# Block-causal attention followed by a gated MLP: V loaded in f32 and cast on Pool, weights issued in pieces, the last key block as a full tile

## Chip, cores and metric

One core of a Trainium2 chip. The metric is the device time of one execution in microseconds. The kernel before: 418.41 us (median of 3 runs, 418.2 to 418.69).

## The reference

```python
B, H, S, D = 8, 8, 576, 64                     # q, k, v: [8, 8, 576, 64] f32
mask = (arange(S)[:, None] // 64) >= (arange(S)[None, :] // 64)
attn = softmax(where(mask, q @ k.T / 8, -1e9)) # rows of a block of 64 see whole blocks
x = (attn @ v).transpose(0, 2, 1, 3).reshape(4608, 512)
h = x @ w_in                                   # w_in [512, 2048]
g = h * sigmoid(beta * h)                      # beta [2048]
out = g @ w_out                                # w_out [2048, 512], out [4608, 512] f32
```

## The kernel before

Work is cut into 32 attention units (a batch has four, each a pair of heads) and 9 row chunks of the MLP (512 rows each: 64 products with w_in, 64 with w_out). The program plans all of it once, on guessed durations: whenever an engine is free it takes the ready operation with the lowest `prio`. The result is a fixed order for each engine, with semaphores between them. What matters below:

```python
# TensorE takes attention first (prio 10*u + 0..5), MLP products only where none is ready
xp  = P.op("PE", ..., prio=10 * u + 5)                    # unit u, of 32
o   = P.op("PE", 4 * mm(512), fh, ..., prio=1000 + 100 * r + j)        # x @ w_in, row chunk r
o   = P.op("PE", 16 * mm(512), fo, ..., prio=1000 + 100 * r + 16 + w)  # g @ w_out
...
# V of a batch: six transfers by Pool, f32 to bf16 on the way, straight into one of two buffers Vn
for i in range(4):
    g.dma_start(Vn[t.slot][:, i, h0:h1, 0:64], v[b, h0:h1, 128*i:128*i+128, :].rearrange("h p d -> p h d"))
...
# E * V of one head: 15 products; the last key block (64 keys) uses smaller tiles
for i in range(5):
    for t in range(i + 1):
        m = 64 if i == 4 and t else 128
        r = slice(64*h, 64*h+64) if t == 4 else slice(0, 128)
        g.matmul(PS[0:m, ..., 65*i:65*i+65], eblk(te, t, i, h), Vn[Tv.slot][r, t, 2*c+h, 0:65], ...)
```

Q and K come by the SP queue in f32, through four staging buffers each, and are cast by Pool (DVE for batch 0). E holds the exponentiated scores; the unit's E*V product is the last big TensorE step of its attention.

The softmax here doesn't subtract the row's maximum and nothing guards it: scores larger than these inputs give would overflow.

## Time and profile before

| | before |
|---|---|
| median, span of the profiled execution | 418.41 us, 413.8 us |
| first E*V product, first MLP product | 28.47 us, 54.09 us |
| w_out landed | 70.4 us |
| E*V of unit 32 starts | 219.0 us |

The page, the stages of the start and the chain are in the prediction. One more view is needed later, busy time by stage; columns: window, length, busy time of PE, PEld, DVE, ACT and Pool with instruction counts, granted clock, DMA share (it can read above 1.00 and is used for comparison only), GB/s.

```profile
72.00:100.00 28.00, 27.38 (x293) 16.34 (x294) 9.57 (x25) 11.79 (x18) 11.88 (x22) 1.00 0.95 108
100.00:130.00 30.00, 28.52 (x398) 18.26 (x399) 21.61 (x50) 23.72 (x33) 20.93 (x42) 1.00 0.76 150
130.00:160.00 30.00, 28.43 (x429) 19.18 (x432) 22.06 (x55) 21.31 (x30) 23.83 (x44) 1.00 1.03 152
```

TensorE is busy for 84.3 of these 88 us, with the DMA engines at 0.76 to 1.03 beside it.

### The profile page before, as it was taken

The numbers are of one execution on the slowest core, as the hardware profiler recorded it, in microseconds if no ns is written. First come the engines' busy times: TensorE is split into PE (matmuls) and PEld (weight loads), VectorE is DVE, ScalarE is ACT, GpSimd is POOL, SyncE is SP. The second block draws the span as 40 slices with busy tenths as digits, with TensorE's granted clock in tenths as the row PEclk, the third lists the DMA queues.
The fourth block names the chain that finished last, engine by engine and source line by source line (L and its number), as shares of the span: only waits on it lengthen the run. The fifth ranks groups of instructions, "written<-read, shape, count | busy, mean of one in ns | idle before, by whom it ended". The sixth has DMA issues, their size and how long they took to land.

```text
span 413.8 us, 7477 instructions
## 1 busy us (share of the span) xinstructions
PE 379.6 (92%) x3006; PEld 201.5 (49%) x3041; DVE 195.7 (47%) x377; ACT 215.2 (52%) x309; POOL 129.6 (31%) x248
## 2 busy tenths in 40 slices
PE   2359998999999998999999999999999999999986
PEld 1136643565655665455555444444444444444432
DVE  2515567244768776683337407137054071370520
ACT  1143676236786766943485437256174272461721
POOL 8366789226678967930010000000000000000000
PEclk9999999999999999999999999999999999999999
DMA  7998999939497999900100020110100101101001
GB/s 179 253 224 174 191 220 187 96 109 141 121 140 205 158 136 202 78 2 27 53 25 2 27 77 0 53 51 2 76 26 27 76 0 52 51 2 76 25 28 76
DMA packets 60899, 37.73 MB, mean 91 GB/s; under 512 B 39856, under 2 KB 56256, under 8 KB 60864
## 3 DMA queue, kind: packets, MB, share of 16 engines
q0 software_dynamic: 42336, 8.92, 24.9%
q1 hardware_dynamic: 18528, 28.33, 23.2%
q8 instruction: 24, 0.39, 0.4%
q14 instruction: 11, 0.09, 0.1%
HBM read 36.71 MB, written 9.44 MB: 112 GB/s over the span
## 4 chain that ended last, share of the span: by engine, by line
PE 74%; ACT 10%; DMA 6%; DVE 4%; POOL 3%; issue 2%; POOLq 0%
PE PS L551 30%; PE PS L531 25%; PE PS L482 11%; ACT E L444 8%; DMA Vn<-in_v_dram 5%; PE PS L437 4%; PE PS L408 2%; PE PS L510 2%; ACT th L539 2%; DMA w_out<-in_moe_w_out_dram 2%; DVE xq L501 1%; POOL w_out L351 1%; DVE gT L543 1%; POOL Vn L370 1%; DVE QT L416 1%
## 5 line engine op out<-in xcount | busy, mean ns | idle before, releaser
L543 DVE SCALAR_TENSOR_TENSOR gT<-th,PS 128x512 bf16<-128x512 f32 x144 | 98.6, 687 | 118.2 <-ACT th L539 118.1
L531 PE MATMUL PS<-xT,w_in 128*128 128x512 bf16 x557 | 127.2, 381 | 2.8 <-DVE KT L416 0.9
L444 ACT ACTIVATE E<-PS 128x1024 bf16<-128x1024 f32 x96 | 94.8, 1034 | 67.1 <-PE PS L437 66.9
L551 PE MATMUL PS<-w_out,gT 128*128 128x512 bf16 x560 | 124.8, 379 | 4.8 <-issue 1.5
L539 ACT ACTIVATE th<-PS,beta 128x512 f32<-128x512 f32 x144 | 99.3, 693 | 27.9 <-PE PS L531 27.9
L551 PEld LDWEIGHTS PS<-w_out,gT 128*128 128x128 bf16 x576 | 55.7, 98 | 70.5 <-issue 2.0
L531 PEld LDWEIGHTS PS<-xT,w_in 128*128 128x128 bf16 x576 | 54.7, 98 | 66.7 <-issue 2.0
L560 ACT ACTIVATE ost<-PS 128x512 f32<-128x512 f32 x36 | 21.5, 597 | 100.4 <-PE PS L551 100.4
L482 PE MATMUL PS<-Vn,E 128*128 128x65 bf16 (+1 forms) x896 | 48.8, 202 | 5.4 <-DMA Vn<-in_v_dram 3.8
L482 PEld LDWEIGHTS PS<-Vn,E 128*128 128x128 bf16 (+1 forms) x896 | 38.4, 104 | 16.0 <-issue 5.4
L437 PE MATMUL PS<-QT,KT 64*128 64x64 bf16 (+5 forms) x384 | 41.6, 310 | 2.2 <-ACT E L444 1.4
L370 POOL DMA_DIRECT2D Vn<-in_v_dram x36 | 31.2, 905 | 7.5 <-PE PS L482 6.5
L450 POOL MEMSET E<- 64x128 bf16 x64 | 13.2, 206 | 54.0 <-ACT E L444 49.2
L501 DVE TENSOR_TENSOR xq<-PS,inv 128x320 bf16<-128x320 f32 x64 | 29.3, 486 | 0.0
L416 DVE COPY QT<-PS 128x576 bf16<-128x576 bf16 x32 | 24.1, 752 | 6.4 <-PE PS L408 5.9
L516 DVE COPY xT<-PS 128x576 bf16<-128x576 bf16 x32 | 14.5, 453 | 26.2 <-PE PS L510 26.1
L402 POOL CAST Qn<-Qs 96x768 bf16<-96x768 f32 x28 | 23.1, 824 | 9.7 <-PE PS L408 8.1
L493 DVE RECIPROCAL inv<-PS 128x5 f32<-128x5 f32 x64 | 8.4, 173 | 36.3 <-PE PS L482 35.9
L437 PEld LDWEIGHTS PS<-QT,KT 64*128 64x128 bf16 (+1 forms) x384 | 14.9, 100 | 21.0 <-issue 7.3
L416 DVE COPY KT<-PS 128x576 bf16<-128x576 bf16 x32 | 24.0, 750 | 1.9 <-PE PS L408 1.7
L402 POOL CAST Kn<-Ks 96x768 bf16<-96x768 f32 x28 | 23.1, 824 | 1.8
L408 PE MATMUL PS<-identB,Kn 96*128 96x96 bf16 x192 | 15.8, 227 | 7.8 <-DVE KT L416 4.6
(27 smaller groups left out, 142.9 us busy)
## 6 DMA issues: line engine op xcount, KB each, us to landing
Qs<-in_q_dram SPq DMA_DIRECT2D x32, 288.0 KB, 4.4
Ks<-in_k_dram SPq DMA_DIRECT2D x32, 288.0 KB, 4.5
out_dram<-ost SPq DMA_DIRECT2D x36, 256.0 KB, 2.0
Vn<-in_v_dram POOLq DMA_DIRECT2D x28, 128.0 KB, 4.1
w_in<-in_moe_w_in_dram POOLq DMA_DIRECT2D x16, 128.0 KB, 6.9
w_out<-in_moe_w_out_dram POOLq DMA_DIRECT2D x16, 128.0 KB, 5.0
Vn<-in_v_dram POOLq DMA_DIRECT2D x8, 64.0 KB, 16.9
Vn<-in_v_dram POOLq DMA_DIRECT2D x14, 32.0 KB, 3.3
```

Source lines behind the costliest of these rows:

```text
L370: z.append(g.dma_start(Vn[t.slot][:, i, h0:h1, 0:64], v[b, h0:h1, 128 * i:128 * i + 128, :].rearrange("h p d -> p h d")))
L402: return g.tensor_copy(nat[tn.slot][:], raw_[ts.slot][:].rearrange("p h j d -> p j h d"))
L408: z = g.transpose(PSb[:, pt.slot, 96 * i:96 * i + 96], nat[tn.slot][:, i, :, :].rearrange("p h d -> p (h d)"), identB[0:96, 0:96])
L416: return g.tensor_copy(dst[td.slot][:].rearrange("c (p j) -> c p j", j=6), PSb[:, pt.slot, 0:576].rearrange("c (j p) -> c p j", j=6))
L437: z = g.matmul(o, KT[tk.slot][r, 128 * t:128 * t + m], QT[tq.slot][r, q0:q1])
L444: return g.activation(E3[te.slot][:, g0, :, :], PS[:, ps.slot:ps.slot + 2, :], ACT.Exp, scale=0.125)
L482: z = g.matmul(o, eblk(te, t, i, h), Vn[Tv.slot][r, t, 2 * c + h, 0:65], start=(t == 0), stop=(t == i or (i == 4 and t == 0)), skip_group_ ...
L501: return g.tensor_tensor(xq[tx.slot][:, :, 64 * w:64 * w + 64], a, x, ALU.mult)
L531: z = g.matmul(PS[:, ph.slot, :], w_in[:, c, 128 * j:128 * j + 128], xT[:, c, row:row + RC], start=(c == 0), stop=(c == 3))
L539: return g.activation(th[tt.slot][:], PS[:, ph.slot, :], ACT.Tanh, scale=beta[:, j:j + 1])
L543: return g.scalar_tensor_tensor(out=gT[tg.slot][:, j, :], in0=th[tt.slot][:], scalar=1.0, in1=PS[:, ph.slot, :], op0=ALU.add, op1=ALU.mult)
L551: z = g.matmul(PS[:, po.slot, :], gT[tg.slot][:, j, 128 * w:128 * w + 128], w_out[:, j, :], start=(j == 0), stop=(j == NJ - 1))
```

## The change

The intent: start earlier (V no longer on Pool's queue, where it crept in beside Q and K; the loads in one queue; the weights behind the first Q, K, V), make E*V shorter (all 15 products in one tile shape), and let the first output rows follow w_out as it lands. The diff, cut:

```diff
+        Vs = [sb(f"Vs{i}", [128, 5, 8, 64], f32) for i in range(NQ)]
...
-                o = P.op("POOL", c, fv, deps=ones, tiles=[t], lat=c + 3000, prio=20 if b == 0 else 50 + b, ...)
+                o = ld["V", b, h0] = P.op("SP", 6 * 400, fv, deps=vzero, tiles=[ts], xfer=5000 * n,
+                         prio=(0.5 if h0 == 0 else 2.5) if b == 0 else 4 * b + 0.5 - 3 * (b > 1), ...)
+                def fw(g, e, ts=ts, t=t, h0=h0, h1=h1):
+                    return g.tensor_copy(Vn[t.slot][:, :, h0:h1, 0:64], Vs[ts.slot][:, :, h0:h1, :])
+                o = P.op("POOL", 300 + 2140 * n, fw, deps=[o, *ones], tiles=[ts, t], ...)
...
-                            m = 64 if i == 4 and t else 128
-                            r = slice(64 * h, 64 * h + 64) if t == 4 else slice(0, 128)
+                            o = PS[:, (pa if h == 0 else pb).slot, 65 * i:65 * i + 65]
+                            z = g.matmul(o, eblk(te, t, i, h), Vn[Tv.slot][:, t, 2 * c + h, 0:65],
+                                         start=(t == 0), stop=(t == i))
...
+        for w in win:  w.deps += [ld["Q", 3], ld["K", 3]]      # one issue per piece of 256 KB
+        for w in wout: w.deps += [ld["Q", 6], ld["K", 6]]
+        for u in range(4, NU):                                 # later Q, K, V wait for weight pieces
+            w = win[4:8] if u < 8 else wout[8:12]
+            for o in [ld["Q", u], ld["K", u]] + ([ld["V", u // 4, 0]] if u % 4 == 0 else []):
+                o.deps += w
...
+                parts = [(0, NJ)] if r or w > 2 else [(4 * a, 4 * a + 4) for a in range(4)]
```

The plan also models the transfers as one queue, so every engine's order changes. (Not in the diff's words, but of weight below: a V can now wait in Vs as well as in Vn, so up to four batches of V can be on the core, and from batch 2 on the `prio` of V puts it ahead of Q and K of the last two units of the batch before.)

## The prediction

> **What bounds the kernel now.** I read the page first (busy shares and slices), then a table by stage, then the chain of waits, then the time line of single products.
>
> ```profile
> span 413.8 us, 7477 instructions
> ...
> PE 379.6 (92%) x3006; PEld 201.5 (49%) x3041; DVE 195.7 (47%) x377; ACT 215.2 (52%) x309; POOL 129.6 (31%) x248
> ...
> PE   2359998999999998999999999999999999999986
> ...
> DMA  7998999939497999900100020110100101101001
> ```
>
> TensorE is full from the fourth slice (about 31 us) to the end; the DMA engines are full only in the first seventeen slices. So there are two places for a gain: how early TensorE gets going, and how much TensorE work there is. The stages, with columns length, busy time of PE, PEld, DVE, ACT and Pool, clock, DMA share and GB/s:
>
> ```profile
> 0.00:28.50 28.50, 9.06 (x77) 4.96 (x77) 10.51 (x17) 7.34 (x10) 19.22 (x40) 1.00 1.18 216
> 28.50:54.00 25.50, 25.25 (x250) 16.59 (x252) 13.30 (x30) 12.63 (x17) 16.26 (x34) 1.00 1.00 192
> ...
> 100.00:170.00 70.00, 65.25 (x948) 43.08 (x952) 50.35 (x120) 51.39 (x72) 52.63 (x97) 1.00 0.93 158
> ...
> 224.00:318.00 94.00, 93.53 (x429) 42.55 (x436) 40.28 (x59) 47.04 (x70) 0.00 (x0) 1.00 0.09 34
> ```
>
> The first 28.5 us hold only 9 us of TensorE work. The chain says what it waits for (start, length, what):
>
> ```profile
> 8.51 19.82 DMA Vn<-in_v_dram
> 28.33 0.14 issue
> 28.47 2.47 PE PS L482 x30
> ...
> 60.48 3.59 POOL w_out L351 x7
> 64.06 6.30 DMA w_out<-in_moe_w_out_dram
> 70.37 1.42 issue
> 71.78 3.40 PE PS L551 x15
> ```
>
> V is the gate of the start: its last piece, issued at 8.51, lands 19.82 us later. Then the E*V products (L482) run, the first MLP product (L531) comes at 54.09, and w_out, landing at 70.37, costs one more small wait. The second place is inside L482:
>
> ```profile
> 28.47 1.07 PE L482 MATMUL PS<-Vn,E 128*128 128x65 bf16 x14 [3.85 <-DMA Vn<-in_v_dram]
> 29.47 0.26 PE L482 MATMUL PS<-Vn,F 64*64 64x65 bf16 x1
> 29.66 1.09 PE L482 MATMUL PS<-Vn,E 128*128 128x65 bf16 x14
> ...
> 128.69 0.72 PE L482 MATMUL PS<-Vn,E 128*128 128x65 bf16 x14
> 129.34 0.21 PE L482 MATMUL PS<-Vn,F 64*64 64x65 bf16 x1
> 129.49 0.72 PE L482 MATMUL PS<-Vn,E 128*128 128x65 bf16 x14
> ```
>
> A head's 15 products take 129.49-128.69 = 0.80 us. The start times of single matmuls in this trace (56 such heads, 72 to 224 us) split it: ten steps of 31 ns from full tile to full tile, 124 ns from the last full tile to the first 64-column one, two steps of 44 ns, 123 ns into the 64x64 tile, 147 ns out of it: 311+124+88+123+147 = 793 ns. Before 54 us the same steps are 54, 175, 65, 174 and 193 ns: 1.21 us.
>
> **What the Trainium skill says.** (1) TensorEngine Tiling (Array Packing), Key Properties: changing the tiling mode drains TensorE. The trace agrees: the three mode changes of a head cost about 93, 92 and 116 ns over a plain 31 ns step. (2) TensorE: Matmul & The Clock Gate, Back-to-back issue gap: N/2.4+2.5 ns warm and N/1.2 ns cold, for 65 columns 29.6 and 54.2 ns. Both are in the trace (29 to 31, and 54). The page's warm-up after about 3.4 us of sustained work does not fit: from 28.5 to 54 us there is hardly a gap, yet the steps stay cold until the 512-column products start. The granted clock reads 1.00 throughout and does not show it. (3) DMA: Bandwidth & Descriptors, Queues, rings and completion order: each DMA engine takes queues in turn, packet by packet. The trace agrees that it hurts V: it writes 128-byte packets on the Pool queue beside 1536-byte packets of Q and K on the SP queue, so V got 0.04 of about 0.48 MB in a 2 us slice from 12 to 22 us. (4) Same page, SWDGE vs HWDGE vs iDMA: a cast during a transfer is possible only from Pool. So V on the SP queue must come as f32 and be cast by an engine.
>
> **The change, part by part.** *V by SP, cast on Pool.* Removed from Pool: 54 issues of V, 31.2+12.0 = 43 us. Added: a cast of 128x2560 per batch. The Q/K cast takes 824 ns for 768 columns, so 2560 take 2.75 us by the same slope; 8 batches make 22 us. Pool ends 21 us lighter, off the critical path. The transfer: Q, K and V become one queue in the order needed: Q0 K0, V of two heads, Q1 K1 Q2 K2, the rest of V, Q3 K3, and the weights only after that. Q0 and K0 landed at 4.57 and 5.59 us; undisturbed Q/K pieces of 0.295 MB landed every 1.1 to 1.3 us. V of two heads is one such piece (6.9 us), the rest of V is three. Alone on the engines (70 to 76 us) 128-byte packets moved 155 GB/s; at the same packet rate 256-byte ones would move 310, so V should be no worse than Q/K per byte. Nine pieces after 6.9 us at 1.2 us: K3 lands at 17.7 us. Behind it lie cast, transposes, copy, scores, three exps, products, division and transposes back: 0.6+0.8+0.75+0.6+3.4+1.7+1.4+1.2 = 10.5 us, from the cold times in this trace. The first MLP product comes at about 28 us instead of 54.1, if w_in (issued from 17.7, 16 issues of 0.57 us) has its first quarter by 23 us. That is 26 us of start.
>
> Not all of it is gain. By 54 us the old kernel has done 108 of 384 Q/K transposes and 76 of 384 score products; four units need 48 each. The other 60 and 28 cost 60*52 ns = 3.1 us and about 2.4 us warm and must now come later. Net: 26-5.5 = 20.5 us.
>
> *Full last tile.* The count stays at 30 products per unit; all three mode changes go. A head becomes 15*31 = 467 ns: 326 ns less on each of the 56 heads that ran warm, 18.3 us. Pure TensorE time in a stage where it has 65.25 of 70 us. The eight cold heads (3.2 us) lie in the start and are not counted twice. A full weight load costs nothing more: 101 ns for 128 columns against 105 to 114 for 64, beside the matmul.
>
> *First output rows in four parts, weights in pieces.* Removes the wait at 70.37: 1.4 us. *New memsets* on DVE and Pool: a few times 0.2 us before any data is there.
>
> Against it I set 3 us for new waits: Q/K of batch 1 are held until the second quarter of w_in has landed, and those of batch 2 until the third of w_out. Sum: 413.8-20.5-18.3-1.4+3 = 376.6 us of span. The timed median is 4.6 us above the profiled span (418.41 against 413.8): 381 us; I say 382.
>
> **Rivals.** (a) *Other engines become the bound of the attention stage.* From 100 to 170 us 457 products are 15.2 units of 4.6 us; with PE at 4.0 us a unit, DVE (3.3) and ACT (3.4) would be at 83 to 85%. For it: they are close, and the chain has 8.2% on the exps. Against it: MLP products fill any hole, and the output ones ask little of either. If the whole tile gain drowned: 400. (b) *DMA becomes the bound.* V as f32 is written at twice the bytes; a unit moves 0.885 MB, 221 GB/s at 4.0 us, and the start moved 232. Against it: a batch unlocks some 12 us of attention and 31 us of MLP for about 15 us of DMA, so only the first 70 us can starve: 12 MB (weights and batch 1) after 18 us at 230 GB/s land at 70, and the work unlocked by then (two input halves of 13.8 us and batch 1) lasts from 28 to about 68. If 256-byte packets move at only 155 GB/s, V takes 7.6 us a batch, and with the starving the result is 388 to 395. (c) *The start is given back*: the fixed order, planned on guessed landing times, makes TensorE, or Pool ahead of its weight issues, wait for the wrong thing, as K2's transposes held the first scores until 18.9 us here. Half the start lost: 392.
>
> **Range and chances.** The tile gain is measured step by step and sits on the bound; the start has the error. Centre 382; 374 if products warm earlier or waits are less, 395 if (b) or (c) takes half of the start. Even (a) stays over 2% ahead, so slower needs something unforeseen. Faster 0.95, same 0.035, slower 0.015.
>
> **What would show it.** Right: L482 in one form of 128*128, two heads in about 0.95 us warm; the first L482 near 12 us and first L531 near 28; w_out landed by about 55 us and no wait there; Pool near 108 us busy; TensorE's idle time after the first MLP product no more than before. Wrong: first L531 after 34 us; V landings of 7 us or more a batch; holes in TensorE between 30 and 70 us that end on Qs, Ks or w_out; L482 steps over 40 ns.

## The result, and the profile after

404.09 us (median of 4 runs, 402.52 to 405.02) against 418.31 (416.26 to 418.69) in the same rounds. Ratio 0.9666, 95% interval 0.9622 to 0.971: faster by 3.3%. Ratios are the mean time of one kernel's runs over that of the other's of the same rounds, so not quite the ratio of the medians quoted. Executions over 1.5% slower than the fastest of the same kernel are left out of the means. The direction was right; the time lies 9 us above the predicted range. The gain in span is 11.3 us where 37 were predicted.

The page after, and its groups of the new products and casts:

```profile
PE 365.3 (91%) x3003; PEld 188.3 (47%) x3041; DVE 196.2 (49%) x380; ACT 214.8 (53%) x308; POOL 107.4 (27%) x212
...
PE   3866999977988898899999999999999999999986
...
PEclk9985899988989999999999999999999999999999
DMA  6899989999999997000110110200100201102002
GB/s 176 178 137 211 216 119 206 231 255 261 241 202 272 214 261 182 2 2 2 51 56 2 52 52 2 78 26 28 73 6 28 78 2 52 52 2 78 26 29 78
...
L503 PE MATMUL PS<-Vn,E 128*128 128x65 bf16 x960 | 36.6, 198 | 8.0 <-POOL E L476 5.6
...
L402 POOL CAST Vn<-Vs 128x2560 bf16<-128x2560 f32 (+2 forms) x9 | 18.7, 2080 | 12.4 <-DMA Vs<-in_v_dram 12.1
```

The predicted pieces are there: one product form, Pool at 107.4 us (predicted 108). But the PE row has 7s and 8s from the 9th to the 17th slice, where nearly all were 9s before, and the clock row dips. By stage:

```profile
28.50:54.00 25.50, 19.83 (x110) 8.86 (x109) 12.30 (x22) 10.83 (x17) 10.32 (x16) 0.73 0.95 185
...
72.00:100.00 28.00, 23.17 (x276) 13.41 (x278) 13.74 (x34) 12.72 (x18) 16.19 (x24) 0.90 1.04 253
100.00:130.00 30.00, 25.92 (x391) 16.20 (x390) 20.69 (x49) 23.13 (x32) 19.70 (x35) 0.92 1.02 236
130.00:160.00 30.00, 26.90 (x461) 17.57 (x463) 22.68 (x55) 23.94 (x34) 22.15 (x41) 1.00 0.94 223
```

From 72 to 160 us TensorE is busy for 76.0 of 88 us, 8.3 less than before, part of it at half clock; the DMA engines are full and move 223 to 253 GB/s. The start, in TensorE's time line (start, length, instructions, and in brackets the wait before them):

```profile
13.71 1.83 PE L503 MATMUL PS<-Vn,E 128*128 128x65 bf16 x30
...
31.73 3.19 PE L560 MATMUL PS<-xT,w_in 128*128 128x512 bf16 x7 [0.95 <-DVE xT L536]
37.94 0.66 PE L432 MATMUL PS<-identB,Qn 96*128 96x96 bf16 x6 [3.02 <-POOL Qn L426]
38.40 3.61 PE L560 MATMUL PS<-xT,w_in 128*128 128x512 bf16 x8
...
47.45 3.63 PE L560 MATMUL PS<-xT,w_in 128*128 128x512 bf16 x16
```

E*V begins 14.8 us earlier than before and the MLP 22.4 us earlier. But eight MLP products take 3.61 us at 38.40, where sixteen take 3.63 at 47.45: half clock, recorded from 29.63 to 43.28 us.

**Where the time went.** Take the start of the E*V product of units 8, 16, 24 and 32 from the trace, and, from the fixed instruction order, how many of the 1152 MLP products stand before it. An MLP product takes 216 ns at full clock (the median step in these traces); deduct that, and what is left is the time each eight units of attention cost beyond the MLP work done meanwhile. For example units 9 to 16 before: 130.3-90.3 = 40.0 us with 152-112 = 40 products (8.6 us) between: 31.4 us. The four stages and the tail add up to the span less 248.8 us of MLP. Each run has one profile; those of e1, e2 and e5 are of their quickest execution, that of e8 of its slowest.

| net us | units 1-8 | 9-16 | 17-24 | 25-32 | tail | span | MLP products before unit 32 |
|---|---|---|---|---|---|---|---|
| before | 66.1 | 31.4 | 30.6 | 29.6 | 7.3 | 413.8 | 284 |
| after | 51.3 | 39.7 | 30.5 | 25.9 | 6.3 | 402.5 | 188 |
| gain | 14.8 | -8.3 | 0.1 | 3.7 | 1.0 | 11.3 | |
| predicted gain | 24.5 | 5.2 | 5.2 | 5.2 | 0 | 37.1 with -3 for waits | |

The predicted gains by stage are the prediction's own terms: 20.5 for the start, 1.4 for w_out, and 0.326 us for each head from unit 5 on (8 heads in the first column, 16 in each other). Attention now ends 31 us sooner, but with 96 fewer MLP products done by then, which is 20.7 us given back. The largest miss is units 9 to 16, which became slower. That is where to look.

What stands in the SP queue there (start, time in the queue's issuing, what):

```profile
71.53 6.25 SPq L388 DMA_DIRECT2D Vs<-in_v_dram  x4
77.82 1.78 SPq L392 DMA_DIRECT2D Vs<-in_v_dram  x2
...
80.29 0.43 SPq L420 DMA_DIRECT2D Qs<-in_q_dram  x1
80.76 0.47 SPq L420 DMA_DIRECT2D Ks<-in_k_dram  x1
...
83.34 6.15 SPq L388 DMA_DIRECT2D Vs<-in_v_dram  x4
89.54 1.78 SPq L392 DMA_DIRECT2D Vs<-in_v_dram  x2
...
94.47 6.51 SPq L388 DMA_DIRECT2D Vs<-in_v_dram  x4
101.02 1.52 SPq L392 DMA_DIRECT2D Vs<-in_v_dram  x2
```

SP spends 24 of the 31 us from 71.5 to 102.5 on issuing V of batches 3, 4 and 5 (batches counted from 0, units from 1); only four pairs of Q and K go out between them, two after each of the first two V. V of batch 3 lands at 81.9 us and is first used at 108.9; V of batch 4 at 93.8 and 127.3; V of batch 5 at 104.7 and 143.1. V of batch 5, first used by unit 21, is issued ahead of Q and K of units 15 to 20. The K of unit 17, first of batch 4, lands only at 113.2. By then five V batches beyond batch 0 have landed, where three were needed. The chain of waits of this stage goes three times through a Q or K load (start, length):

```profile
80.29 4.91 DMA Qs<-in_q_dram
...
105.92 8.56 DMA Qs<-in_q_dram
...
120.21 5.29 DMA Ks<-in_k_dram
```

That is 18.8 us. Between 72 and 160 us the chains of before, e4 and e5 hold no load at all, that of e11 one K of 5.74 us, that of e18 one K of 9.43 us.

### The profile page after: what moved, and what is told of

Same layout as the page of the kernel before. It is cut to its first block, busy times and chain, and to the rows that moved or that the text cites. A ratio compares the mean times of both kernels' runs of the same rounds, so it can differ in the third digit from the quotient of the medians.

```text
span 402.5 us, 7496 instructions
## 1 busy us (share of the span) xinstructions
PE 365.3 (91%) x3003; PEld 188.3 (47%) x3041; DVE 196.2 (49%) x380; ACT 214.8 (53%) x308; POOL 107.4 (27%) x212
## 2 busy tenths in 40 slices
DMA packets 60899, 42.45 MB, mean 105 GB/s; under 512 B 39856, under 2 KB 56256, under 8 KB 60864
## 4 chain that ended last, share of the span: by engine, by line
PE 67%; DMA 9%; ACT 8%; DVE 6%; POOL 4%; SPq 3%; issue 2%; POOLq 0%
PE PS L584 30%; PE PS L560 27%; ACT E L468 6%; DMA Qs<-in_q_dram 6%; PE PS L503 5%; PE PS L461 2%; PE PS L432 2%; SPq L388 2%; DMA w_in<-in_moe_w_in_dram 1%; DVE gT L572 1%; DVE xq L521 1%; DMA Ks<-in_k_dram 1%; POOL Kn L426 1%; ACT th L568 1%; POOL Qn L426 1%
## 5 line engine op out<-in xcount | busy, mean ns | idle before, releaser
L560 PE MATMUL PS<-xT,w_in 128*128 128x512 bf16 x553 | 131.4, 390 | 3.6 <-DVE xT L536 1.0
L560 PEld LDWEIGHTS PS<-xT,w_in 128*128 128x128 bf16 x576 | 55.8, 100 | 68.6 <-issue 5.1
L595 ACT ACTIVATE ost<-PS 128x512 f32<-128x512 f32 x35 | 20.9, 597 | 101.7 <-PE PS L584 96.7
L461 PE MATMUL PS<-QT,KT 64*128 64x448 bf16 (+5 forms) x384 | 41.9, 298 | 4.6 <-ACT E L468 1.4
L503 PE MATMUL PS<-Vn,E 128*128 128x65 bf16 x960 | 36.6, 198 | 8.0 <-POOL E L476 5.6
L503 PEld LDWEIGHTS PS<-Vn,E 128*128 128x128 bf16 x960 | 33.0, 100 | 15.3 <-POOL E L476 7.9
L440 DVE COPY QT<-PS 128x576 bf16<-128x576 bf16 x32 | 24.0, 750 | 10.2 <-PE PS L432 9.9
L426 POOL CAST Qn<-Qs 96x768 bf16<-96x768 f32 x28 | 23.1, 824 | 14.8 <-DMA Qs<-in_q_dram 12.9
L432 PE MATMUL PS<-identB,Qn 96*128 96x96 bf16 x192 | 15.0, 220 | 12.6 <-POOL Vn L350 4.7
L402 POOL CAST Vn<-Vs 128x2560 bf16<-128x2560 f32 (+2 forms) x9 | 18.7, 2080 | 12.4 <-DMA Vs<-in_v_dram 12.1
L474 POOL MEMSET E<- 64x128 bf16 x64 | 13.0, 203 | 29.6 <-ACT E L468 24.4
```

Source lines behind the costliest of these rows:

```text
L426: return g.tensor_copy(nat[tn.slot][:], raw_[ts.slot][:].rearrange("p h j d -> p j h d"))
L432: z = g.transpose(PSb[:, pt.slot, 96 * i:96 * i + 96], nat[tn.slot][:, i, :, :].rearrange("p h d -> p (h d)"), identB[0:96, 0:96])
L440: return g.tensor_copy(dst[td.slot][:].rearrange("c (p j) -> c p j", j=6), PSb[:, pt.slot, 0:576].rearrange("c (j p) -> c p j", j=6))
L461: z = g.matmul(o, KT[tk.slot][r, 128 * t:128 * t + m], QT[tq.slot][r, q0:q1])
L503: z = g.matmul(o, eblk(te, t, i, h), Vn[Tv.slot][:, t, 2 * c + h, 0:65], start=(t == 0), stop=(t == i))
L560: z = g.matmul(PS[:, ph.slot, :], w_in[:, c, 128 * j:128 * j + 128], xT[:, c, row:row + RC], start=(c == 0), stop=(c == 3))
```

## The experiments

Theories, as they stood before the runs: **A**, the two gains are there and a new wait eats them; **B**, the shorter products were never on the path. Later: **V**, the new route of V costs (its bytes, its cast, its queue, or its place in it); **O**, the fixed order of TensorE, attention first, leaves too little MLP beside the loads; **C**, the half clock. "Exact order" means that each engine's instruction order is that of the kernel named, instruction by instruction. Gains by stage are computed as in the table above, against before.

**e1_tile_alone.** Before's exact order, with the full tile alone.

```diff
-  m = 64 if i == 4 and t else 128            # before
+  o = PS[:, slot, 65*i:65*i+65]; g.matmul(o, eblk(...), Vn[Tv.slot][:, t, 2*c+h, 0:65], ...)
+  # Vn and E padded with zeros for the last 64 keys
```

> The kernel before, in its own instruction order on all engines, with only the full last tile (plus a few memsets at the start). Theory A (the tile gain is real TensorE time, and the changed kernel lost other time to waits for Q, K and V): 418.3 less 56 warm heads of 0.326 us and 8 cold ones of 0.4 us, 21 us, of which at most 3 turn into new waits: 397 to 400 us. Theory B (ACT, DVE or the loads bind the attention stage, so that less TensorE work there buys little): 408 to 416 us.

406.97 us (404.91 to 408.52), ratio 0.9757 [0.9694, 0.9819], correct. Between the two theories. By stage 3.2, 2.8, 1.2, 3.0: 10.2 us of the 18.3 came through. Its two longest waits for loads (columns: waiter, releaser, total us, times, longest):

```profile
PE PS L494 <- DMA Vn<-in_v_dram: 7.4, 1, 7.4
PE PS L562 <- DMA w_out<-in_moe_w_out_dram: 6.2, 1, 6.2
```

The first lies before the first E*V product, where the tile can't act. The second was 1.55 us before: TensorE reached w_out sooner and waited for it.

**e2_old_tiles.** The changed kernel's exact order, with the old tile mix.

```diff
+  m = 64 if i == 4 and t else 128            # in the changed kernel
```

> The changed kernel in its own instruction order on all engines, with the old mix of tile shapes. Theory A (in its attention stage TensorE stands waiting for loads part of the time, so longer products fill waits first): 6 to 14 us over the changed kernel, 410 to 418 us. Theory B (TensorE is the bound there, the waits lie elsewhere): the full 18 to 21 us, 422 to 425 us.

412.11 us (408.46 to 414.52), 0.9876 [0.9799, 0.9953]: inside A's range, 8 us above the changed kernel in the medians (4.2 in the spans of the profiled runs; that of e2 was its quickest, so half of the difference has no stage). Unit 24 starts at 157.6 us against 156.9: up to there the shorter products changed nothing that the end can see; only units 25 to 32 differ by 2.9 us.

**e3_no_gate.** Q, K and V no longer wait for weight pieces.

```diff
-        for u in range(4, NU): ...  o.deps += w
```

> The changed kernel without the waits that hold Q, K and V of batch 1 behind the second quarter of w_in and those of batch 2 on behind the third of w_out (the plan's order shifts with it). Theory A (the sum of bytes is what is late): loads only change places, 400 to 408 us. Theory C (these holds starve TensorE at 30 to 38 us and 77 to 92 us): the 6 us hole at 30 us and the half-clock stretch behind it go, 388 to 396 us.

408.17 us, 0.9794: worse than the change. One wait of 15.9 us for a Q cast appears in the start (gain there 2.0 instead of 14.8). Units 9 to 16 cost 31.5 us net instead of 39.7, but units 1 to 16 together 95.6 instead of 91.0: the loss changed places. Holding Q and K behind the weights is not the fault in sum.

**e4_v_sixth.** The changed kernel's exact order, with one of the six V transfers of batches 2 to 7. Its output is wrong, which doesn't matter for the time.

```diff
-  for i in range(4): ...   for o in range(2): ...
+  for i in range(4 if b < 2 else 1): ...   for o in range(2 if b < 2 else 0): ...
```

> The changed kernel in its own instruction order, but V of batches 2 to 7 is only loaded to one sixth of its transfers (wrong result on purpose): 5.9 MB less to load. Theory A (loads bind the attention stage, waits on Q and K from 72 to 130 us and the half-clock windows they cause): those waits shrink, 388 to 396 us, last Q or K landed before 140 us instead of 161. Theory C or a plan that is wrong for another reason: 401 to 405 us.

395.5 us (394.03 to 396.29), 0.9484: 8.6 us better than the change. Units 9 to 16 cost 32.5 us net instead of 39.7, and the other stages hardly move. (The pages differ by 5.5 MB, not the 5.9 that was expected.) So at this order most of V's loading costs 7 us, all of it in units 9 to 16.

**e5_spread.** No load touched: the products of a row chunk get a rank among the six attention units that follow its inputs, instead of coming after all attention. Correct.

```diff
+  def mp(r, x): return 10 * (4 * ((RC * r + RC - 1) // S + 1) + 6 * x / 20) + 6
-  prio=1000 + 100 * r + j
+  prio=mp(r, j)
```

> The changed kernel with one number changed in its planning: the products of MLP chunk r are ranked among the attention of the batches that follow, instead of behind all attention. Loads, tiles and bytes are the same. Theory A (loads bind the attention stage because attention is ordered ahead of MLP work that could fill): the waits on Q and K between 72 and 170 us and the half-clock windows there go, 10 to 18 us less than the changed kernel, 386 to 394 us, with TensorE over 97% busy after 90 us. Theory D (TensorE can't be filled there, for lack of PSUM banks or because ACT and DVE bind): 400 to 406 us.

393.43 us (390.5 to 394.69), 0.9414: 10.7 us better than the change, from the plan's order alone. The SP queue issues its loads in the same order up to Q and K of unit 18, and no byte less. Up to unit 8 nothing differs (124 products before it in both); then 316 products stand before unit 16 instead of 156. Net units 9 to 16 cost 30.8, units 17 to 24 27.4 us. TensorE stays busy:

```profile
72.00:100.00 28.00, 26.54 (x260) 13.73 (x257) 16.64 (x35) 15.88 (x24) 15.59 (x24) 0.94 1.11 260
100.00:130.00 30.00, 29.76 (x300) 16.40 (x301) 18.06 (x39) 18.03 (x26) 9.40 (x16) 1.00 0.82 203
130.00:160.00 30.00, 29.43 (x282) 15.31 (x281) 17.97 (x36) 22.13 (x32) 11.76 (x21) 1.00 0.40 98
```

85.7 of 88 us, against 76.0. Up to 100 us the DMA engines are as full as in the change, yet no load stands in the chain of waits between 72 and 160 us.

**e6_spread_cal.** e5 with the plan's durations set to the measured ones.

```diff
-  av = P.op("PE", 30 * 46, ...)   xfer=5000, 1050, 880     # V, Q/K, weights
+  av = P.op("PE", 30 * 33, ...)   xfer=5400, 1150, 1100    # and 5 units for 6 in mp
```

> As the one before, with the plan's durations set to what the changed kernel's trace shows (products 33 ns a step, V 5.4 us, Q and K 1.15 us, weights 1.1 us). Theory A: within 3 us of the one before, as the order in the middle is not sensitive to the guesses any more; the start up to 72 us is no better, since it waits for bytes. If the guesses were the fault: 5 us or more better.

399.38 us, 0.9549: a miss. Better guesses made a worse order; 4.9 us of the loss against e5 are in the start.

**e7_warm.** The second MLP group of the start is computed three times, to fill the 3.02 us wait and keep the clock up.

```diff
-  for c in range(4):
+  for c in list(range(4)) * (3 if row == 0 and j == 1 else 1):
```

> The changed kernel in its own order, with the second group of the first MLP chunk (4 products) done three times over, same result, so that TensorE works where it waited for Q from 34.9 to 37.9 us. Theory E (the half clock from 29.6 to 43.3 us follows from that idle time and costs as such): full clock from about 36.5 us, the 16 products after it at 216 instead of 430 ns, 2 to 4 us less than the changed kernel. If the waits alone matter: no change or up to 1 us more.

403.96 us (6 runs), 0.9665: no gain. Full clock came back at 35.88 instead of 43.28 us and unit 8 came 1.8 us sooner, but unit 24 started at 157.3 us (after: 156.9). What the start won, units 9 to 16 lost again. Theory C falls for the half clock of the start; the shorter stretches of half clock after 84 us were not tested apart from the waits before them.

**e8_v_pool.** The changed kernel with V loaded as before: by Pool, cast in the transfer, no Vs. Correct.

```diff
-  o = P.op("SP", 6 * 400, fv, deps=vzero, tiles=[ts], xfer=5000 * n, ...)   # and the cast fw
+  o = P.op("POOL", 6 * 900, fv, deps=[*vzero, *ones], tiles=[t], xfer=5000 * n, ...)
```

> The changed kernel with V loaded as before (issued by Pool, cast in the transfer, no cast on Pool); order of the loads, weights and tiles as in the change, though the plan's order shifts. Theory A: from 100 us on fewer bytes are written, and waits there shrink, but at the start V of two heads is slower against Q and K: 398 to 408 us. If f32 V by SP is the gain of the change: 412 us or more. If it is its loss: 392 us or less.

386.51 us (384.91 to 390.19), 0.927 [0.9217, 0.9324]: 17.6 us better. Against the change, units 1 to 8 gain 3.6, units 9 to 16 7.6, units 17 to 24 1.6, units 25 to 32 1.3 us (14.1 in all; the profiled execution was the slowest). But the plan's order differs too: 256 products instead of 188 stand before unit 32.

**e9_v_bytes.** e8's exact order, V of batches 2 to 7 written in f32 into a buffer that nothing reads. Its output is wrong, which doesn't matter for the time.

```diff
+  V_ = Vn[t.slot] if b < 2 else Vs[t.slot]
```

> e8_v_pool in its own instruction order, but V of batches 2 to 7 is written as f32, 256 bytes a packet, into a buffer that nobody reads (wrong result on purpose; still issued by Pool, still no cast by an engine). If the bytes of f32 V are what the change lost by: 4 to 9 us over e8_v_pool, 391 to 396 us. If it is V's place in the SP queue and the cast that waits for it: within 2 us of e8_v_pool, 385 to 389 us.

386.29 us, 0.9256: as e8. But the packets were not the 256 bytes expected: without a cast, Pool's queue moved this V in packets of 4096 bytes by the trace (12,209 packets under 512 bytes in the whole run, against 39,856 in e8 and in the change). So e9 alone does not show what f32 V costs; e18, with 39,856 again, does.

**e10_v_pool_spread.** e8 with e5's ranks. Correct.

> e8_v_pool and e5_spread together (V by Pool in bf16, MLP products ranked among the attention). If both took away the same waits in the attention stage, it is little better than the better one, 383 to 387 us; if each took away its own, up to 8 us more, 377 to 382 us. TensorE over 98% busy after 75 us either way.

383.17 us (381.95 to 383.56), 0.9173 [0.9131, 0.9215]: the best version found, 20.9 us better than the change.

```profile
72.00:100.00 28.00, 26.78 (x277) 13.98 (x276) 18.54 (x37) 22.00 (x32) 14.32 (x28) 1.00 0.93 170
100.00:130.00 30.00, 30.00 (x263) 15.27 (x260) 13.74 (x30) 14.83 (x23) 9.78 (x18) 1.00 0.52 86
130.00:160.00 30.00, 29.44 (x304) 16.07 (x303) 20.11 (x41) 19.19 (x28) 13.86 (x24) 1.00 0.64 117
```

TensorE is busy for 86.2 of 88 us at full clock. The two remedies do not add up (17.6 and 10.7 give 20.9): they mend the same loss.

**e11_v_late.** The changed kernel with V placed later in the queue. The plan shifts. Correct.

```diff
-  4 * b + 0.5 - 3 * (b > 1)
+  4 * b + 2.5
```

> The changed kernel with V's place in the SP queue moved back: behind Q and K of the second unit after its batch's first, where the change puts V of batches 2 on ahead of the Q and K of the batch before; bytes, cast and tiles are the same (the plan's order shifts). If V's place in the queue is the loss: 8 to 15 us under the changed kernel, 389 to 396 us. If bytes or the cast are: 400 to 408 us.

402.42 us (401.35 to 405.27), 0.965: hardly better in sum, but the stages say why. Units 9 to 16 cost 30.8 us net instead of 39.7 (K of unit 17 lands at 101.1 instead of 113.2); the start loses 2.0, units 17 to 24 2.8 and units 25 to 32 1.2 us, where the new order has 148, 152 and 180 products before units 16, 24 and 32 and TensorE waits 11.7 us, nine times, for the zeroing of E on Pool.

**e12_v_f32_pool.** V in f32 issued by Pool, then cast. The plan shifts. Correct.

```diff
-  o = P.op("SP", 6 * 400, fv, ...)
+  o = P.op("POOL", 6 * 900, fv, ...)
```

> The changed kernel with V still f32 and cast on Pool, but issued by Pool, so that it is a queue of its own beside Q and K (the plan's order shifts, and its start is later, as it counts 5.4 us of issue before the first cast). If the SP queue's order is the loss: 388 to 396 us in spite of it. If bytes and cast are: 402 us or more.

408.92 us, 0.9792: TensorE waits 8.9 us for the first cast; the start gains only 3.8. Its V, too, went in 4096-byte packets. Units 9 to 16 cost 32.8 us net, but units 1 to 16 together 95.1, 4.1 more than in the change, so it does not settle the later batches.

**e13_cast_short, e14_cast_no_wait, e15_cast_dve.** Three ways to take the cast off Pool's back: the changed kernel's exact order with the cast of batches 2 to 7 cut to one column; with that cast reading a constant and not waiting for V (both wrong on purpose); and the cast on DVE (correct).

```diff
+  if b > 1: return g.tensor_copy(Vn[t.slot][:, 0, 0, 0:64], Vs[ts.slot][:, 0, 0, :])   # e13
+  if b > 1: x = <constant>;  o.free_of = ov    # e14: the wait for V is left out, nothing is read of it
-  o = P.op("POOL", 300 + 2140 * n, fw, ...)    # e15
+  o = P.op("DVE", 200 + 1700 * n, fw, ...)
```

> The changed kernel in its own instruction order on all engines, with the cast of V of batches 2 to 7 cut to one column of 64 (wrong result on purpose): it still waits for V, but takes 0.1 us instead of 2.3. Theory F (Pool, which works in order, stands in the way of PV: waiting for V in front of the E memsets and the Q and K casts): 0 to 3 us less than the changed kernel, 401 to 404 us. Theory G (the time of the cast itself on Pool is the loss): 8 us or more less, 396 us or under.

> The same order again, with the cast of V of batches 2 to 7 at full length but reading a constant instead of V, so that it waits for no load (wrong result on purpose); V is still loaded. Theory F: Pool's 12 us of waiting for V go, 5 to 10 us less than the changed kernel, 394 to 399 us. Theory G or the place of V in the SP queue ahead of Q and K: 401 to 404 us.

> The changed kernel with the cast of V on DVE instead of Pool, everything else alike (the plan's order shifts a little; correct result). Theory F in the form that any engine working in order is held up: DVE waits for V in front of copies that PV and the scores need, 400 to 408 us. If Pool is the wrong engine for it because its time is short: 394 to 399 us.

403.76, 405.06 and 407.32 us (6 runs each; ratios 0.9723, 0.9744, 0.9775). Neither the cast's length nor its waiting is the loss. In all three unit 24 starts at 156.2 to 157.8 us.

**e16_best.** e10 with E*V products planned at 33 ns.

```diff
-  av = P.op("PE", 30 * 46, ...)
+  av = P.op("PE", 30 * 33, ...)
```

> The combination that the runs so far point to: full tile, weights and output rows as in the change, V by Pool in bf16 as before, MLP products ranked among the attention, products planned at 33 ns. Against e10_v_pool_spread it has the last point more: 376 to 383 us; nothing would show if TensorE is as full already, 382 to 384 us.

385.93 us, 0.9266: not better than e10. A miss.

**e17_v_own_queue and e18_v_in_sp.** The same step in both directions, V of batches 1 to 7 moved between the SP queue and Pool's at fixed order, each at its planned time. e17 starts from e13, e18 from e9. Their outputs are wrong, which doesn't matter for the times.

```diff
+  for o in [ld["V", b, 0] for b in range(1, B)]:
+      P.order["SP"].remove(o); o.eng = "POOL"; P.order["POOL"].insert(k, o)     # e17; e18 the reverse
```

> The order of instructions of e13_cast_short on every engine (that is the changed kernel with the cast of batches 2 to 7 cut to one column), with one thing moved: the loads of V of batches 1 to 7 are issued by Pool instead of SP, each at the planned time it had, still f32, still the same bytes and packets. Wrong result on purpose for batches 2 to 7. Theory Q (V's place in the one queue with Q and K makes the following Q, K and weights late): 388 to 396 us, and the Q and K pieces of batch 2 issued and landed at least 5 us earlier than in the changed kernel. Theory O (the order of the instructions in the plan is what separates the changed kernel from e8_v_pool): 401 to 406 us, as e13_cast_short (403.8).

> The opposite step: the order of instructions of e9_v_bytes (386.3 us, V on its own queue, f32, batches 2 to 7 to a buffer that nothing reads), with the loads of V of batches 1 to 7 moved from Pool to the SP queue, each at the planned time it had. Wrong result on purpose for batches 1 to 7. Nothing waits for these loads; only what stands behind them in the SP queue can be later. Theory Q: 396 to 403 us. Theory O: 385 to 389 us, as e9_v_bytes.

e17: 418.07 us (414.67 to 418.84), 1.0014 [0.9963, 1.0065]; 14 us worse, outside both theories. Its Pool now issues V between the casts, columns as in the time lines:

```profile
88.17 1.78 POOL L388 DMA_DIRECT2D Vs<-in_v_dram  x2
94.08 1.75 POOL L388 DMA_DIRECT2D Vs<-in_v_dram  x2 [4.14 <-issue]
95.83 1.25 POOL L392 DMA_DIRECT2D Vs<-in_v_dram  x2
97.11 0.46 POOL L476 MEMSET E<- 64x128 bf16 x2
97.64 0.82 POOL L428 CAST Kn<-Ks 96x768 bf16<-96x768 f32 x1
```

The K cast behind them came late, and TensorE waited for it:

```profile
PE PS L434 <- POOL Kn L428: 6.7, 2, 6.2
```

So e17 burdened Pool, and its V on Pool went in 4096-byte packets, not in the same ones as expected; it is no clean test of the queue. What it does show: V still came early (batch 5 landed at 104.1 and was used at 158.5), and units 9 to 16 were not mended by another queue (net 44.3 us).

e18: 386.87 us (386.58 to 389.36), 0.9294 [0.9255, 0.9333], as e9: **V in the SP queue, with all its bytes and in 256-byte packets, costs nothing at this order** (it has no cast, and no product waits for V). The theory that the shared queue is itself the loss falls. SP is held by V just as long:

```profile
72.63 7.88 SPq L389 DMA_DIRECT2D Vs<-in_v_dram  x4
...
96.69 8.52 SPq L389 DMA_DIRECT2D Vs<-in_v_dram  x4
```

The difference is when: between these two, seven pairs of Q and K go out, V of batches 3 and 4 lands at 83.9 and 109.3, 12.8 and 6.1 us before the products that would need it, and K of unit 17 lands at 95.3. Three V batches beyond batch 0 have landed by then, not five.

## Why the prediction was wrong

**The step that failed** is in rival (b): "a batch unlocks some 12 us of attention and 31 us of MLP for about 15 us of DMA, so only the first 70 us can starve", with its twin in (a), "MLP products fill any hole". The work was unlocked, but it was not in the order. TensorE runs a fixed, attention-first order: from unit 8 to unit 24 only 40 MLP products stand in it, 8.6 us, beside four batches whose Q, K and V take 15 us each. So attention ran at the pace of the loads or of its own chain. Changes to TensorE's or Pool's work did not move the start of unit 24: old tiles 157.6 us, a warmer start 157.3, a short cast 157.5, a cast on DVE 157.8, the change itself 156.9. Less V data did (e4, 147.6). And with MLP work put in between (e5), 10.7 us came back with the same bytes to load. This is shown.

**A second step failed with it**: "Q, K and V become one queue in the order needed". From batch 2 on it is not. V's `prio` puts it ahead of two units of the batch before, and two more buffers let it run up to six units ahead of its own Q and K, so that in units 9 to 16, where loads bind (18.8 us of Q and K in the chain), Q and K wait behind V that is needed 27 to 38 us later. Two batches too many, at 4.7 to 5.3 us each from the last K landed before them to their own landing, are an estimate of 10 us; less V data (e4) gave back 7.2, a later place for V (e11) 8.9, and e18 with V just in time costs 31.6 against 39.7, all net in units 9 to 16. e4 holds the order fixed but is a smaller load, e11 is a later place but the plan shifts, e18 has another order; no run moves V later at the changed kernel's exact order, so the size is not settled to better than that. Excluded are V's bytes and its queue as such (e18, at its order) and the cast (e13 to e15); the gates are not the fault in sum (e3).

**By stage.** Of the 25.8 us that were missing, 13.5 are units 9 to 16 (both steps above).

The start is 9.7 us short. First E*V at 13.71 us (near 12 was predicted) and K3 at 18.4 (17.7) were right; the first MLP product came at 31.73 instead of 28 (3.7 us), and some 19 products then ran at 430 ns instead of 216 (4.1 us, an estimate from those steps): the kernel before recorded full clock from 56.76 us on, 2.7 us after its first product. The rest, 2 us, is left open. e8, e9, e10 and e18 gained 18.4 to 22.2 there, so a start of the predicted size was to be had. But these four load the first V by Pool, as before (first E*V at 15.5 to 16.6 us): V's move to SP, on which the prediction rested, is not needed for it. What is left of the change there is the order of the loads (two heads of V first, later Q and K and the weights behind), and no run takes that apart.

In units 17 to 24 the tile's 5.2 us are gone (-5.1) although loads no longer lag there: 8 MLP products stand beside eight units, where e5 and e10 (256 products) and e18 (48) gain 3 us and e8 and e9 (48) 1.7. That is rival (a) in part: attention alone cannot use a faster TensorE. Which of its other engines sets that pace is open. Units 25 to 32 gained 3.7 of 5.2, of which e2 puts 2.9 down to the tile.

**The tile** itself was sized well: about 31 ns a step within a head (31 predicted), one form, two heads in 1.06 us (about 0.95 predicted). What was wrong is that it counted "in a stage where it has 65.25 of 70 us": TensorE being busy 93% of a stage did not mean that its time was all on the path, since e1, with nothing else changed, got 10.2 of 18.3.

The 3 us "for new waits" was the one term for all this. w_out landed at 66.3 us instead of by 55, held behind Q and K of unit 7, which stood behind V of batch 1. The timing constant was also off: 4.6 us from span to median held 2.8 us of chance, since the profiled execution of before was a quick one (415.65 us); that raised the prediction, so it hid a little of the miss by luck.

**Right:** Pool lighter (107.4 us); V's 4.7 to 5.3 us a batch by SP (batches 3 to 5), under the 7 us that would have been wrong; no wait left for w_out; faster at all. That Pool's work is off the critical path was not quite right: it is 4% of the chain after, 3% before.

The predicted time was to be had: with V as before, e8 needs 386.5, and with the MLP spread (e10) 383.2, against 382 predicted.

## What to carry to other kernels

Count what stands beside a load-bound stage in the order that will really run: work that is unlocked hides no load if a fixed order puts it after. When a new staging buffer lets one stream run further ahead, look at what it overtakes; here V's being early was not free, at a DMA share of 0.94 to 1.04 from 72 to 160 us. Measure a gain to a fixed point of the work (here a unit, with the filler done so far deducted): it shows in which stage it is lost when the total shows only that it is.

## What the Trainium skill lacked or had wrong

- TensorE: Matmul & The Clock Gate, What's actually happening: the clock halves after at least one idle window of about 3.4 us and comes back after a busy one; the windows are free-running. The way back fits: in the changed kernel products ran back to back from 38.40 us, and full clock came at 43.28 us, at the end of the first wholly busy window (39.87 to 43.28 us). The half-clock stretches after 84 us last one window each (84.24 to 87.65, 97.89 to 101.31, 114.96 to 118.37 us, 3.41 each). What does not fit is how they begin: no window was idle. In the 3.41 us before each, TensorE was busy for 1.77, 1.11 and 2.23 us. And the kernel before ran its small products cold from 28.5 to 54 us with hardly a gap; the page gives no rule for those.
- DMA: Bandwidth & Descriptors, Rules for kernel authors: spreading DMAs over issuing engines does not help bandwidth and only saves issue time, and a DMA should be issued early and waited for late. No run here tests the first as such: e18 and e9 take the same time from either queue (386.87 and 386.29 us), but not in the same packets. What the page lacks is two sizes. Issue time: a V transfer held Pool for 0.89 us (24.8 us for 28 in e17), and four of a whole batch in a row held SP for 3.5 to 10 us (3.49 in the change, 10.15 in e11), with every Q and K behind them. And the price of early: V landed 27 to 38 us before its use in units 13 to 24, and units 9 to 16 took 8.3 us longer than before; no page says what early costs once the DMA engines are full.
- No page says that a cast changes the packets: V went in packets of 128 bytes with the cast on Pool's queue (e8), of 4096 bytes without it (e9), of 256 bytes from SP (e18).
- No page treats how much other work a fixed order should put beside a load-bound stage: 10.7 us between the changed kernel and e5.
